# Moving five weight subtractions to GpSimd and a late table and its gathers into the first layer of expert 0

## The chip, the cores and the metric

The kernel runs on one core of a Trainium2 chip. The metric is the device time of one execution in microseconds. Five engines work side by side, each through its own instructions in order: PE (TensorE), DVE (VectorE), ACT (ScalarE), POOL (GpSimd) and SP (SyncE, which here only issues transfers). They wait for one another through semaphores.

## The reference, cut to what matters

```
state = gamma * state + k_t v_t          # retention: 4 batches, 8 heads, 768 steps, 64 wide
y_t   = scale * q_t . state
x     = y, as 3072 tokens x 512          # the input of the expert layer
e(token)    = argmax over 8 experts of the normalised logits
gate(token) = softmax weight of that expert
out[token]  = gate * ( relu(x @ w1[e]) @ w2[e] )     # w1 512x1024, w2 1024x512
```

All of it is float32; each expert works on the tokens that chose it.

## The kernel before, in words

**Retention.** Twelve blocks of 256 tokens (`m` = 0 to 11) run one after the other. In a block PE transposes the next block's q and k into PSUM, forms scores, and adds products into the two PSUM banks `py`; ACT copies the transposes to SBUF (`copy_k`, `transpose_q`) and `take(m)` copies the two banks to `yT` with three copies on ACT (L470, L473 twice). `rows(m)` turns `yT` on DVE (L478, tile `x`) and SP stores it to `xd` in HBM with four transfers (L485). `logits_products` and `logits_rows` make the expert logits of the block.

**Routing.** Blocks come in four groups of three. For a group, `sums`, `choose`, `count`, `ranks` find expert and rank of each token on DVE and PE; `split_ranks`, `marks_of`, `mark` build one-hot marks on DVE; `table` (L617) multiplies the marks on PE and DVE adds the result to `tab`, the list of tokens by expert. `counting` sorts the seven other experts by their number of tokens (`perm`, `cnti`); `sorted_tables` turns `tab` into the indices `gi` and `ri` (L716 to L729) with which GpSimd gathers rows of `xd` by indirect DMA (`gather`, L661).

**Experts.** Expert 0 is fixed as the first. Its first 288 tokens (`EARLY`) come from the first three groups and are gathered during block 10 (`early_gather`, `xge`); the other 128 (`late`) are gathered after the last table into `xr0`, together with all rows of the first sorted expert (`gather_rows(1)`), which go by `write_rows` to HBM and come back turned by `read_quarters` (`xg`), then through DVE and ACT (`x_turn`, `x_low`) to PE. Before the gathers `xr0` is cleared on POOL (L1189); it lies in memory that the retention's tiles give back.

**Weights.** Each expert's weights come in 8 pieces of 128x1024 (four of `w1`, four of `w2`) into 4 buffers `raw`. `split_cast` casts a piece to `whi` on ACT (L229) and returns a function that writes the low part `wlo = raw - whi` (L234); `split` does both. PE takes three products per matrix step, whi.xh, whi.xl, wlo.xh. `first_layer` of expert 0 is 8 times 12 products; a generator, `run(n)`, lets n of them into PE's order, so that the last group's routing stands between them. `hidden` gives `hh` (ACT, L253) and `hl` (DVE, L256); the first two `hl` are kept back in `held`. `layer2` is 24 products for each of four output parts (L1124); its step kt takes `hh`, `hl` number kt and piece 4 + kt/2.

**What sets the order.** Each engine's order is the order in which the program issues (a manual schedule). The places of the change: the branch of block 10 (`m == NM - 2`, L921 to L943) and of block 11 (L959 to L963), the end of a block (L964 to L979), the code after the blocks from L1003 on, and the start of the expert part from L1179 on.

Of the kernel before, what the change touches and what calls it, by code (L numbers as in the profile page):

```python
# [24 lines left out]
P = 128  # L25
# [7 lines left out]
NE = 8  # L33
# [78 lines left out]
def retention_moe(ctx: ExitStack, tc: tile.TileContext, q, k, v, emb, tau, w1, w2, const, const16, out):  # L112
# [351 lines left out]

    def take(m):
        yTs[m] = ap_.tile([P, KT, T2], F32, name="yT", bufs=3)
        y = yTs[m].rearrange("p (i j) (u c) -> p i (j u) c", i=2, u=2)
        at = (slice(0, 4, 2), slice(1, 4, 2)) if m % NCB else (slice(0, 4, 3), slice(1, 3))
        py = [t.rearrange("p (i j) c -> p i j c", i=2) for t in pys[m]]
        nc.scalar.copy(out=y[:, :, at[0]], in_=py[0])  # L470
        for o in range(2):

            nc.scalar.copy(out=y[o * D:(o + 1) * D, :, at[1]], in_=py[1][(1 - o) * D:(2 - o) * D])  # L473

# [236 lines left out]
    M = NE - 1  # L711
    perm = cp.tile([P, M, M], F32, name="perm")

    def sorted_tables():

        nc.vector.tensor_copy(out=ri[:, 0, 3:], in_=tab[:, 0, 2:3])  # L716
        nc.vector.tensor_copy(out=ri[:Q, 0, 3:], in_=tab[:Q, 0, 3:])
        yield
        w = ap_.tile([P, KT * P], F32, name="pm01", bufs=1)
        w = w[:, :M * NG * M].rearrange("p (m j e) -> p m j e", m=M, j=NG)  # L720
        nc.vector.tensor_tensor(out=w, in0=perm.unsqueeze(2).broadcast_to([P, M, NG, M]),
                                in1=tab[:, 1:].rearrange("p e j -> p j e").unsqueeze(1).broadcast_to([P, M, NG, M]),
                                op=ALU.mult)
        yield
        nc.vector.tensor_reduce(out=tsort, in_=w, axis=AX.X, op=ALU.add)
        yield
        nc.vector.tensor_scalar(out=gi[:, 1:], in0=tsort, scalar1=float(NT - 1), scalar2=None, op0=ALU.min)
        yield
        nc.vector.tensor_copy(out=ri[:, 1:], in_=tsort)  # L729
        yield  # L730

    def counting():
# [11 lines left out]
        yield  # L744
        pos = cp.tile([P, M], F32, name="pos")
        nc.vector.tensor_reduce(out=pos, in_=gt3, axis=AX.X, op=ALU.add)
        yield
# [107 lines left out]
    for m in range(NM):  # L855
# [3 lines left out]
        py_of(m)  # L859
        if m == NM - 2:  # L860
            first = [split_cast()]

        if m == 0:
# [36 lines left out]
        else:  # L900
# [8 lines left out]
            if urgent:  # L909
                rows(m - 1)  # L910
            if m == NM - 2:
                mark(tail - 1, range(6))
            logits_rows(m - 1, logits_products(m - 1))
            if nxt:
# [3 lines left out]
                if m == NM - 2:  # L918
# [3 lines left out]
                    state_sums(m + 1)  # L922
                    first[0]()
                transpose_q(m + 1, 0)
# [10 lines left out]
                if m == NM - 2:  # L935
                    split_cast()()
                    spread_v(m + 1, 0)
# [21 lines left out]
            else:  # L959
                lows[0]()  # L960
                intra(m, 0)
                lows[1]()
                intra(m, 1)  # L963
                ps = [turn_rows(xge, EROWS, kt, bank(f"pst{kt}")) for kt in range(2)]  # L964
        waiting = done
        take(m)
        if m < NM - 2:
            spread_v(m + 1, 0)
            spread_v(m + 1, 1)
        if m == NM - 2:  # L970
            spread_v(m + 1, 1)
            lows = [split_cast(), split_cast()]
        if m == 0:
            next(emb_steps)
        if m == NM - 1:
            xh0, xl0 = (hp.tile([P, KT, CAP], F32R, name=n) for n in ("xh", "xl"))
            for kt in range(KT):
                rows_T(xge, EROWS, kt, slice(0, EARLY), ps[kt] if kt < 2 else None)
            nc.gpsimd.tensor_copy(out=zs[0][:, :3], in_=xge[:, :, DM:DM + NE])  # L979

# [18 lines left out]
    def run(n):  # L999
        for _ in range(n):  # L1000
            next(todo, None)
# [3 lines left out]
    logits_rows(m, pl)  # L1005
    rows(m - 2)
    load_piece()
    load_piece()
    run(11)
    for j, n in EROWS[:2]:  # L1010
        square(xge, n, j, j)
    first_low = split_cast()
    z = sums(g)
    run_all(choose(g, z))
    run_all(add_counts(g, z))
    rows(m - 1)
    put_scores(g)
    run(21)
    pr = count(g)
    sort_steps = counting()  # L1020
    run_all(ranks(g, pr))
    next(sort_steps)
    for o in held:
        o()
    first_low()
    rows(m)
    square(xge, EROWS[2][1], 2, 2)
    for _ in range(9):
        next(sort_steps)
        run(1)  # L1030
    split_ranks(g)
    marks_of(g)
    for i in range(6):
        run(1)
        mark(g, (i,))
    load_expert(1)
    load_piece()
    run(4)
    split()
    load_piece()  # L1040
    load_expert(2)
    run(12)
    split()
    run(12)
    split()
    load_piece()
    load_piece()
    run(DF)
    turn_of[:] = ["b2", "b3"]

# [127 lines left out]

    def last_table():  # L1179
        table(tail)  # L1180
        run_all(sorted_tables())

    acc = layer2(0, 0, hh0, hl0, EARLY, between=last_table)
    ctxa.close()
# [7 lines left out]
    nc.gpsimd.tensor_copy(out=zs[0][:, 3], in_=xr0[:, 0, DM:DM + NE])  # L1192
    late = slice(EARLY, CAPS[0])

    def turn_late():
# [9 lines left out]
    for dt in range(3):  # L1205
        if dt:
            acc = layer2(0, dt, hh0, hl0, EARLY, between=turn_late if dt == 2 else None)
        y_turn(dt, acc, yt0, EARLY)
# [269 lines left out]
```

## Time and profile before

| what | us |
|---|---|
| median of 3 runs (lowest, highest) | 398.46 (397.87, 399.46) |
| the profiled execution, its own time | 400.53 |
| its span, first to last instruction | 398.8 |
| PE busy in the span | 386.0 |
| DVE, ACT, POOL busy | 250.2, 226.9, 125.7 |

The profiled execution took 2.07 us more than the median of the three runs; 1.73 us of it lie outside its span. A timeline row gives the start, the length, engine, line, operation, output and inputs, and in brackets the idle time in front of it with what ended it. Lengths overlap in a pipeline: two products of 288 columns that follow without a wait start 0.133 us apart though each is listed with 0.29.

### The profile page before, as it was taken

Reading aid. Unit: us, or ns where it says so; the run is one execution under the profiler, and the core shown is the slowest. Engines: PE = TensorE matmul, PEld = TensorE weight load, DVE = VectorE, ACT = ScalarE, POOL = GpSimd, SP = SyncE. Lnnn points to the kernel's source line nnn. Section 1 sums busy time; section 2 is a strip of 40 time slices with the busy share of each in tenths; the row PEclk is TensorE's granted clock in tenths of the full one; section 3 lists DMA queues with packets and bytes.
Section 4 is the critical chain, followed back from the end, with each engine's and each line's share of the span. In section 5 each row is a group of like instructions: output and inputs, shape, how many; then the busy total and the mean of one; then the engine's idle time right before and its main releaser. Section 6 shows DMA issues by size and latency. Waiting matters only on the chain.

```text
span 398.8 us, 9514 instructions
## 1 busy us (share of the span) xinstructions
PE 386.0 (97%) x3652; PEld 353.3 (89%) x3652; DVE 250.2 (63%) x564; ACT 226.9 (57%) x402; POOL 125.7 (32%) x142
## 2 busy tenths in 40 slices
PE   7999999999999998999999999999999999999992
PEld 4988888888789886999999999999889889999971
DVE  4655776779799767745773864767366547576400
ACT  5687687887974165455545655734765545453410
POOL 2765644452400434222602712420371052001131
PEclk9999999999999999999999999999999999999998
DMA  8989989999369769596979698696989687933121
GB/s 230 280 267 280 277 255 259 250 268 237 97 188 249 223 184 320 155 259 218 286 220 260 225 292 197 215 316 187 250 281 315 155 265 234 235 120 98 30 100 53
DMA packets 86470, 88.02 MB, mean 221 GB/s; under 512 B 9184, under 2 KB 65120, under 8 KB 86416
## 3 DMA queue, kind: packets, MB, share of 16 engines
q1 hardware_dynamic: 81936, 74.32, 65.8%
q0 software_dynamic: 4304, 12.93, 9.5%
q8 instruction: 31, 0.51, 0.6%
q14 instruction: 23, 0.19, 0.2%
q10 hardware_dynamic: 176, 0.07, 0.1%
HBM read 65.00 MB, written 18.43 MB: 209 GB/s over the span
## 4 chain that ended last, share of the span: by engine, by line
PE 80%; DVE 7%; DMA 6%; issue 2%; ACT 2%; POOL 1%; SPq 1%; POOLq 0%; DVEq 0%; ACTq 0%
PE pst L247 12%; PE b L247 10%; PE py L247 9%; PE py L1124 8%; PE b L1174 7%; PE py L451 7%; PE b L1124 5%; PE b L387 5%; PE pst L1124 4%; PE py L1174 4%; PE pst L421 2%; PE b L356 2%; DMA xd<-x 2%; PE b L374 2%; DMA xg<-xs 2%
## 5 line engine op out<-in xcount | busy, mean ns | idle before, releaser
L234 DVE TENSOR_TENSOR wlo<-raw,whi 128x1024 fp32r<-128x1024 f32 x64 | 78.0, 1221 | 22.8 <-ACT whi L229 17.4
L1156 POOL DMA_INDIRECT out_dram<-og,si x28 | 30.0, 1071 | 125.7 <-ACT og L1149 87.1
L229 ACT CAST whi<-raw 128x1024 fp32r<-128x1024 f32 x64 | 66.3, 1043 | 0.1
L407 DVE TENSOR_TENSOR pm<-b,mask 128x512 f32<-128x512 f32 x48 | 29.8, 684 | 13.1 <-PE b L387 13.0
L1105 DVE STREAM_TRANSPOSE xt<-xg 128x384 f32<-128x384 f32 (+1 forms) x28 | 15.7, 579 | 31.2 <-DMA xg<-xs 31.2
L661 POOL DMA_INDIRECT xr<-xd,gi x24 | 29.8, 1242 | 14.9 <-ACT sq L288 7.7
L350 POOL TENSOR_TENSOR hl<-wlo,cst 128x512 f32<-128x512 f32 x22 | 22.5, 1043 | 36.2 <-DVE pm L407 17.3
L247 PE MATMUL pst<-xl,whi 128*128 128x380 f32 (+7 forms) x96 | 32.4, 337 | 0.7 <-DVE xl L1112 0.7
L247 PE MATMUL pst<-xh,whi 128*128 128x380 f32 (+7 forms) x96 | 32.1, 335 | 0.4 <-ACT xh L1106 0.4
L247 PE MATMUL pst<-xh,wlo 128*128 128x380 f32 (+7 forms) x96 | 32.0, 333 | 0.0
L1106 ACT CAST xh<-xt 128x408 fp32r<-128x408 f32 (+6 forms) x28 | 14.2, 510 | 27.0 <-DVE xt L1105 26.7
L253 ACT ACTIVATE hh<-pst 128x380 fp32r<-128x380 f32 (+7 forms) x24 | 11.6, 484 | 28.1 <-PE pst L247 28.1
L247 PE MATMUL b<-xh,whi 128*128 128x408 f32 (+7 forms) x80 | 26.8, 335 | 0.0
L247 PE MATMUL b<-xl,whi 128*128 128x408 f32 (+7 forms) x80 | 26.7, 333 | 0.0
L247 PE MATMUL b<-xh,wlo 128*128 128x408 f32 (+7 forms) x80 | 26.6, 332 | 0.0
L247 PE MATMUL py<-xh,whi 128*128 128x288 f32 (+7 forms) x80 | 26.3, 329 | 0.0
L247 PE MATMUL py<-xh,wlo 128*128 128x288 f32 (+7 forms) x80 | 26.2, 328 | 0.0
L247 PE MATMUL py<-xl,whi 128*128 128x288 f32 (+7 forms) x80 | 26.2, 327 | 0.0
L273 POOL TENSOR_TENSOR r<-r,half 128x4 f32<-128x4 f32 (+1 forms) x9 | 8.9, 993 | 51.7 <-DVE r L272 51.6
L387 PE MATMUL b<-qT,kT 64*128 64x128 f32 x384 | 24.9, 279 | 0.0
L387 PEld LDWEIGHTS b<-qT,kT 64*128 64x128 f32 x384 | 22.6, 188 | 1.7 <-issue 0.9
L451 PE MATMUL py<-pm,vs 128*64 128x128 f32 x384 | 23.9, 276 | 0.0
(246 smaller groups left out, 1025.7 us busy)
## 6 DMA issues: line engine op xcount, KB each, us to landing
raw<-in_moe_w_dram SPq DMA_DIRECT2D x60, 512.0 KB, 4.9
whi<-in_q_dram SPq DMA_DIRECT2D x24, 256.0 KB, 4.5
xd<-x SPq DMA_DIRECT2D x48, 128.0 KB, 4.6
wlo<-in_k_dram SPq DMA_DIRECT2D x11, 512.0 KB, 5.5
xs<-xr SPq DMA_DIRECT2D x6, 768.0 KB, 4.9
whi<-in_v_dram SPq DMA_DIRECT2D x6, 512.0 KB, 5.7
wlo<-in_v_dram SPq DMA_DIRECT2D x6, 512.0 KB, 6.1
xg<-xs SPq DMA_DIRECT2D x16, 192.0 KB, 4.7
```

What stands on the lines that cost most here:

```text
L229: nc.scalar.copy(out=hv, in_=rv)
L234: eng.tensor_tensor(out=lv, in0=rv, in1=hv.bitcast(F32), op=ALU.subtract)
L247: nc.tensor.matmul(acc[:, :w], a[:, f], x[:, kt, cols], start=(n == 0), stop=(n == 3 * KT - 1))
L350: return eng.tensor_tensor(out=ks_r[:, m % 3, s, h], in0=kin[m % 3][:, h, s], in1=w[:, h], op=ALU.mult)
L387: nc.tensor.matmul(psc[a][:, j], kTs[m][a * D:(a + 1) * D, j, u].rearrange("p s c -> p (s c)"), q_cols(m, a, j, u), start=True, stop=True, ...
L407: o.append(nc.vector.tensor_tensor(out=pm, in0=psc[a], in1=w, op=ALU.mult))
L451: nc.tensor.matmul(pys[m][b][o * D:(o + 1) * D, j], lhsT, rhs, start=first, stop=True, skip_group_check=True)
L661: return nc.gpsimd.indirect_dma_start(out=xr[:n, j, :], out_offset=None, in_=xd[:rows_, :], in_offset=bass.IndirectOffsetOnAxis(ap=gi[:n, ...
L1105: nc.vector.transpose(out=xt[:, :n], in_=xgs[e][:, :n, kt * Q:(kt + 1) * Q])
L1124: nc.tensor.matmul(acc[:, :c], a[:, f], x[:, kt, :c], start=(n == 0), stop=(n == 3 * FT - 1))
L1156: i = nc.gpsimd.indirect_dma_start(out=out[:, :], out_offset=bass.IndirectOffsetOnAxis(ap=si[:n, e, j:j + 1], axis=0), in_=og[:n, j, :], i ...
L1174: nc.tensor.matmul(acc[:s, :], x[:, kt, at], a, start=(n == 0), stop=(n == 3 * FT - 1))
```

## The change

It leaves the arithmetic as it is and changes who does it, and when.

- In blocks 10 and 11 the first expert's piece 0 is cast after block 11's transposes instead of before them; piece 1 is cast after `take(10)`; pieces 1 and 3 get their low parts on POOL. `take(11)` does its two half copies on DVE.
- The low parts of pieces 4, 5 and 6 go to POOL too; piece 2 and piece 7 stay on DVE.
- `rows(9)` moves into block 11, `rows(10)` ahead of the last choice; the marks of the last group come ahead of the held `hl` and of `rows(11)`.
- The last `table` and `sorted_tables` move from the first part of layer 2 (behind its 18th product) to behind the 72nd product of the first layer; the clearing of `xr0` and the five gathers come directly after it. `perm` lies in PSUM now.
- The sort that gives `cnti`, and with it the loads of expert 1's first four pieces, come after the gathers.

```diff
-    def take(m):
+    def take(m, copy=nc.scalar.copy):
...
-            nc.scalar.copy(out=y[o * D:(o + 1) * D, :, at[1]], in_=py[1][(1 - o) * D:(2 - o) * D])
+            copy(out=y[o * D:(o + 1) * D, :, at[1]], in_=py[1][(1 - o) * D:(2 - o) * D])
...
-    perm = cp.tile([P, M, M], F32, name="perm")
+    perms = []
...
+        perm = pc[:, P:P + M * M].rearrange("p (m e) -> p m e", m=M)
+        perms.append(perm)
...
-        if m == NM - 2:
-            first = [split_cast()]
...
+            if not nxt:
+                rows(m - 2)
...
-                    first[0]()
...
-                    split_cast()()
+                    split()
...
-                lows[0]()
+                second_low()
                 intra(m, 0)
-                lows[1]()
                 intra(m, 1)
...
-        take(m)
+        take(m, nc.scalar.copy if nxt else nc.vector.tensor_copy)
...
         if m == NM - 2:
+            split(nc.gpsimd)
             spread_v(m + 1, 1)
-            lows = [split_cast(), split_cast()]
+            second_low = split_cast()
...
         if m == NM - 1:
+            nc.gpsimd.tensor_copy(out=zs[0][:, :3], in_=xge[:, :, DM:DM + NE])
+            split(nc.gpsimd)
...
-    rows(m - 2)
     load_piece()
     load_piece()
+    rows(m - 1)
     run(11)
...
-    first_low = split_cast()
+    turn_of[:] = ["b2", "b3"]
+    split(nc.gpsimd)
     z = sums(g)
...
-    rows(m - 1)
     put_scores(g)
-    run(21)
+    run(16)
     pr = count(g)
     sort_steps = counting()
     run_all(ranks(g, pr))
-    next(sort_steps)
+    for _ in range(5):
+        next(sort_steps)
+    square(xge, EROWS[2][1], 2, 2)
+    split_ranks(g)
+    marks_of(g)
+    mark(g, range(6))
     for o in held:
         o()
-    first_low()
     rows(m)
...
+    run(21)
+    split(nc.gpsimd)
     run(12)
-    split()
+    split(nc.gpsimd)
     run(12)
...
+    last_low = split_cast()
...
-    acc = layer2(0, 0, hh0, hl0, EARLY, between=last_table)
+    table(tail)
+    run_all(sorted_tables())
...
     gather_rows(1)
...
+    run(12)
+    last_low()
+    for _ in range(4):
+        next(sort_steps)
+    load_expert(1)
+    load_piece()
+    load_piece()
+    load_expert(2)
+    load_piece()
+    load_piece()
+    run(DF)
```

ACT, blocks 10 and 11, from the copies of `take(9)` and `spread_v` on (`whi` is a cast piece, `kT` and `qT` the turned k and q, `vs` the spread v). Before:

```order
L400 COPY vs<-whi 64x512 x4
L229 CAST whi<-raw 128x1024
L361 COPY kT<-b_1985 128x8x64
L375 COPY qT<-b_2021 128x512
L375 COPY qT<-b_2027 128x512
L361 COPY kT<-b_2033 128x8x64
L229 CAST whi<-raw 128x1024
L400 COPY vs<-wlo 64x512 x2
L470 COPY yT<-py_1907 128x4x128
L473 COPY yT<-py_1908 64x4x128 x2
```

And with the change:

```order
L400 COPY vs<-whi 64x512 x4
L361 COPY kT<-b_1981 128x8x64
L375 COPY qT<-b_2016 128x512
L375 COPY qT<-b_2022 128x512
L361 COPY kT<-b_2028 128x8x64
L229 CAST whi<-raw 128x1024
L400 COPY vs<-wlo 64x512 x2
L470 COPY yT<-py_1906 128x4x128
L473 COPY yT<-py_1907 64x4x128 x2
L229 CAST whi<-raw 128x1024
```

One of the two casts ahead of `take(10)` has moved behind it.

POOL, from the early gathers of block 10 to the late ones (`zs` are scores of the gathered rows, `xr` the late rows), as a difference:

```order
 L661 DMA xge<-xd,ri 128x520 x2
 L661 DMA xge<-xd,ri 32x520
-L979 COPY zs_82<-xge 128x24
-L1189 MEMSET xr_2490 128x520
-L661 DMA xr_2490<-xd,ri 128x520
+L234 TENSOR_TENSOR wlo<-raw,whi 128x1024
+L976 COPY zs_82<-xge 128x24
+L234 TENSOR_TENSOR wlo<-raw,whi 128x1024
+L234 TENSOR_TENSOR wlo<-raw,whi 128x8x4x32 x3
+L1174 MEMSET xr_2396 128x520
+L661 DMA xr_2396<-xd,ri 128x520
```

Five subtractions of a whole piece stand ahead of the clearing and the late gathers.

DVE, from the last group's marks on (`hl` low parts of the hidden layer, `tab` the table, `ri` indices). Before:

```order
L609 TENSOR_SCALAR pm_2322<-cst_62,low 128x128 x6
L256 SCALAR_TENSOR_TENSOR hl<-pst_2305,hh 128x288
L234 TENSOR_TENSOR wlo<-raw,whi 128x8x4x32
L256 SCALAR_TENSOR_TENSOR hl<-b_2355,hh 128x288
L234 TENSOR_TENSOR wlo<-raw,whi 128x8x4x32
L256 SCALAR_TENSOR_TENSOR hl<-b_2386,hh 128x288
L234 TENSOR_TENSOR wlo<-raw,whi 128x8x4x32
L256 SCALAR_TENSOR_TENSOR hl<-py_2405,hh 128x288
L256 SCALAR_TENSOR_TENSOR hl<-py_2428,hh 128x288
L622 TENSOR_TENSOR tab<-tab,b_2462 128x32
L623 TENSOR_TENSOR tab<-tab,b_2462 128x32
L716 CAST ri<-tab 128x1
```

And with the change:

```order
L609 TENSOR_SCALAR pm_2288<-cst_62,low 128x128 x6
L256 SCALAR_TENSOR_TENSOR hl<-py_2204,hh 128x288
L256 SCALAR_TENSOR_TENSOR hl<-py_2241,hh 128x288
L478 STREAM_TRANSPOSE x<-yT 128x4x4x32 x2
L256 SCALAR_TENSOR_TENSOR hl<-pst_2255,hh 128x288
L256 SCALAR_TENSOR_TENSOR hl<-pst_2320,hh 128x288
L256 SCALAR_TENSOR_TENSOR hl<-b_2339,hh 128x288
L622 TENSOR_TENSOR tab<-tab,b_2374 128x32
L623 TENSOR_TENSOR tab<-tab,b_2374 128x32
L716 CAST ri<-tab 128x1
```

Three subtractions of weights are gone from between marks and table, and the turn of `rows(11)` has come in. The five `hl` there are now the first to the fifth; the other three and one subtraction stand behind the indices.

## Rows read from the trace of the kernel before

**Rows 1.** Timeline of ACT, block 10.

```profile
99.39 1.05 ACT L229 CAST whi<-raw 128x1024 fp32r<-128x1024 f32 x1
```

**Rows 2.** Timeline of PE, block 11 to the first product of expert 0.

```profile
106.71 1.09 PE L451 MATMUL py<-qT,s 64*64 64x128 f32 x28 [0.39 <-ACT yT L473]
...
112.37 0.64 PE L498 MATMUL b<-yT,enT 128*32 128x256 f32 x8
112.94 0.40 PE L247 MATMUL py<-xh,whi 128*128 128x288 f32 x1
```

**Rows 3.** Timeline of PE, layer 2 of expert 0, parts 0 to 2, and what follows.

```profile
126.54 0.30 PE L1124 MATMUL pst<-hh,whi 128*128 128x288 f32 x1
...
129.20 0.40 PE L1124 MATMUL pst<-hh,wlo 128*128 128x288 f32 x1 [0.44 <-DVE wlo L234]
...
131.07 0.40 PE L1124 MATMUL pst<-hl,whi 128*128 128x288 f32 x1 [0.57 <-DVE hl L256]
...
138.74 0.40 PE L1225 MATMUL b<-whi,xh 128*128 128x512 f32 x1
```

**Rows 4.** Timeline of DVE, the last group's ranks, marks and table.

```profile
118.08 0.21 DVE L567 TENSOR_TENSOR rs<-b,oh 128x48 f32<-128x48 f32 x1
...
118.52 0.81 DVE L256 SCALAR_TENSOR_TENSOR hl<-py,hh 128x288 fp32r<-128x288 f32 x2
...
120.38 1.30 DVE L478 STREAM_TRANSPOSE x<-yT 128x512 f32<-128x512 f32 x2
121.60 0.12 DVE L739 SCALAR_TENSOR_TENSOR key<-cnt,cst 128x8 f32<-128x8 f32 x1
...
122.49 0.21 DVE L753 TENSOR_TENSOR gt<-perm,cst 128x49 f32<-128x49 f32 x1
...
123.48 0.16 DVE L579 TENSOR_TENSOR ge<-rank,cst 128x18 f32<-128x18 f32 x1
...
125.09 1.06 DVE L609 TENSOR_SCALAR pm<-cst,low 128x128 f16<-128x128 f16 x6
...
131.30 0.18 DVE L622 TENSOR_TENSOR tab<-tab,b 128x32 f32<-128x32 f32 x1
```

**Rows 5.** Timeline of POOL, clearing and last late gather.

```profile
133.17 0.53 POOL L1189 MEMSET xr<- 128x520 f32 x1 [24.56 <-DMA raw<-in_moe_w_dram]
...
139.26 0.92 POOL L661 DMA_INDIRECT xr<-xd,gi  x1 [0.30 <-issue]
```

**Rows 6.** Chain that ended last, expert 1's rows: start, length, what.

```profile
147.03 6.17 DMA xg<-xs
```

**Rows 7.** Timeline of PE, the start of expert 1.

```profile
153.70 0.40 PE L1174 MATMUL pst<-wlo,hh 128*128 128x512 f32 x1
154.51 0.45 PE L247 MATMUL pst<-xh,whi 128*128 128x408 f32 x1 [0.41 <-ACT xh L1106]
...
158.54 0.35 PE L247 MATMUL b<-xh,whi 128*128 128x408 f32 x1
```

**Rows 8.** The page, part 5: a GpSimd subtraction's nearest relative, busy and mean ns.

```profile
L350 POOL TENSOR_TENSOR hl<-wlo,cst 128x512 f32<-128x512 f32 x22 | 22.5, 1043 | 36.2 <-DVE pm L407 17.3
```

**Rows 9.** Timelines of POOL and of DVE, the same stretch.

```profile
143.22 0.20 POOL L1084 COPY zs<-xr 128x24 f32<-128x24 f32 x1 [1.14 <-DMA xr<-xd,gi]
143.91 0.65 POOL L1086 COPY zs<-xr 32x8 f32<-32x8 f32 x1 [0.49 <-DMA xr<-xd,gi]
...
143.29 1.22 DVE L234 TENSOR_TENSOR wlo<-raw,whi 128x1024 fp32r<-128x1024 f32 x1 [2.35 <-ACT whi L229]
```

**Rows 10.** Timeline of SP: stores of block 11, loads of expert 1.

```profile
121.70 2.62 SPq L485 DMA_DIRECT2D xd<-x  x4
125.46 5.55 SPq L204 DMA_DIRECT2D raw<-in_moe_w_dram  x4
```

**Rows 11.** Tile `xd`: stores issued 115.2 to 116.6, their landing.

```profile
DMA to landing us min/median/max: 2.0/2.1/2.2
```

**Rows 12.** Tile `xd`: stores issued 123.3 to 123.8, their landing.

```profile
DMA to landing us min/median/max: 3.9/3.9/3.9
```

More of the change, by code (lines that the diff above doesn't have):

```diff
@@ L720, in sorted_tables @@
         w = w[:, :M * NG * M].rearrange("p (m j e) -> p m j e", m=M, j=NG)
-        nc.vector.tensor_tensor(out=w, in0=perm.unsqueeze(2).broadcast_to([P, M, NG, M]),
+        nc.vector.tensor_tensor(out=w, in0=perms[0].unsqueeze(2).broadcast_to([P, M, NG, M]),
                                 in1=tab[:, 1:].rearrange("p e j -> p j e").unsqueeze(1).broadcast_to([P, M, NG, M]),
@@ L978, in retention_moe @@
                 rows_T(xge, EROWS, kt, slice(0, EARLY), ps[kt] if kt < 2 else None)
-            nc.gpsimd.tensor_copy(out=zs[0][:, :3], in_=xge[:, :, DM:DM + NE])
         for _ in range(LOADS.count(m)):
@@ L1021, in retention_moe @@
     run_all(ranks(g, pr))
-    next(sort_steps)
+    for _ in range(5):
[4 more added lines that the diff above has]
+    mark(g, range(6))
     for o in held:
         o()
-    first_low()
     rows(m)
[L1027 to L1038, printed above, removed]
-    split()
-    load_piece()
-    load_expert(2)
+    run(21)
+    split(nc.gpsimd)
     run(12)
-    split()
+    split(nc.gpsimd)
     run(12)
[L1045 to L1049, printed above, removed]
+    last_low = split_cast()
     xgs, xTs, xrs = {}, {}, {}
@@ L1176, in layer2_rows @@
         return acc
-    def last_table():
-        table(tail)
-        run_all(sorted_tables())
-    acc = layer2(0, 0, hh0, hl0, EARLY, between=last_table)
+    table(tail)
+    run_all(sorted_tables())
     ctxa.close()
@@ L1205, in retention_moe @@
     for dt in range(3):
-        if dt:
-            acc = layer2(0, dt, hh0, hl0, EARLY, between=turn_late if dt == 2 else None)
+        acc = layer2(0, dt, hh0, hl0, EARLY, between=turn_late if dt == 2 else None)
         y_turn(dt, acc, yt0, EARLY)
```

## The prediction

> **What bounds the kernel now.** I read the page first. PE is busy 386.0 of 398.8 us (the table above), so only time in which PE waits, or work taken off it, can bring anything; this change takes no product off PE. So I went through PE's timeline from block 10 to expert 1 and looked for rows with a bracket, or for starts further apart than 0.133 us. There are three places.
>
> First, ahead of block 11's products PE waits for ACT's copies of `take(10)`: the bracket [rows 2]. ACT is late because two casts of weights stand ahead of those copies; the reader sees the first, 1.05 us, before the copy of `kT` [rows 1].
>
> Second, layer 2 of expert 0. Its first three parts run from 126.54 to 138.74 [rows 3], 12.20 us. They hold 72 products at 0.133 us, 9.60, the four transposes of the late rows, 0.44 with their gap, and the last table, 0.19. That leaves 1.97 us of waiting, shown by the brackets on `wlo` and `hl`, both of DVE. DVE is the late one: between 126.4 and 131.3 it does three weight subtractions with `hl` between them, and then the table.
>
> Third, expert 1. Its first product could follow the row at 153.70 by 0.23 us, at 153.93, and twelve products of 0.184 us would bring the next group to 156.14. It starts at 158.54 [rows 7]: 2.40 us lost, with `xh` and `xl` of expert 1's rows as the releasers. The chain of waits says why: their last transfer lands at 147.03 + 6.17 = 153.20 [rows 6]. Back along it stand the last gather, issued at 139.26, and the clearing of `xr` at 133.17 [rows 5], which starts when DVE has made the indices. So the table's place sets when expert 1 can start.
>
> **The change, part by part.**
>
> *Casts.* One cast of 1.05 us leaves the front of block 11's transposes. PE's transposes were done some 0.2 us before ACT was free to copy them, and that is all that is gained: `take(10)` comes 0.2 us sooner, since its other cast still stands ahead. The first product of expert 0 goes from 112.94 [rows 2] to 112.75.
>
> *`take(11)` on DVE.* The trace has no such copy. The half copies cost 0.58 us each on ACT, and a DVE operation of 512 columns from PSUM is the nearest relative of that size; I take 0.6 each, with 0.58 and 0.7 as ends. ACT's third cast ends near 109.7, DVE's subtraction behind it (1.22 listed [rows 9], 1.15 in a train) at 110.9, the copies at 112.1. The logits start at 112.37 before [rows 2], 112.17 now. So this is hidden with less than 0.1 us to spare, and costs 0 to 0.2.
>
> *Five subtractions on POOL.* The nearest row is a GpSimd subtraction's relative of half the width, 1043 ns [rows 8]; twice that is 2.05 us (lower end 2.0; upper end 2.7, where POOL also waits 0.65 for DVE [rows 9]). The fourth piece is cast by 111.3, so its low part ends at 113.4 and is wanted by the twelfth product at 114.3. Those of pieces 4, 5, 6 run at about 115.0 to 117.0, 119.9 to 121.9, 121.9 to 124.0; layer 2 wants the last at 128.4. All are covered, and POOL had nothing to do there: it waited 24.56 us [rows 5]. At 2.7 us still only the fourth piece comes near its product.
>
> *DVE without them.* From ranks to marks the path is 0.44 (118.08 to 118.52), 0.89 (121.60 to 122.49) and 2.67 (123.48 to 126.15) [rows 4], 4.0 us. Starting at 117.05 the marks end at 121.1. Two `hl` (0.72), the turn of `rows(11)` (1.22) and three `hl` (1.1) follow, to 124.15. PE makes the table after 72 products, at 123.15, so DVE is the later one and starts `tab` at 124.15. Table to indices takes 133.17 - 131.30 = 1.87 [rows 4, 5]: indices at 126.05. Then one `hl`, the one subtraction left (1.15, to 127.6), the sort for `cnti` (to 128.3), the last two `hl` (to 129.1). PE starts layer 2 at 126.54 - 0.2 + 0.19 = 126.53 and wants the sixth `hl` at 128.7 (there at 126.4), the last subtraction at 129.2 and the seventh `hl` at 129.1 (there at 128.65), the eighth at 129.5. So the 1.97 us of waiting go. What is late next is that seventh `hl`, with 0.4 us to spare. Together with the 0.2, PE is 2.15 us ahead at 136.6.
>
> *Gathers.* The clearing also waits for the stores of `rows(11)`, whose tile it overwrites: turned by 123.1, issued within 2.1, landed 2.0 to 3.9 us later [rows 10 to 12]. That gives 127.2 to 129.1. The stores at 115.2 had few others beside them and so do these, whose loads now come later; I take 127.4. The last gather follows 6.09 behind (133.17 to 139.26), at 133.5, and the landing of expert 1's rows 13.94 behind that (139.26 to 153.20), at 147.4, or at 149.1 with the late stores.
>
> *Expert 1.* DVE can turn those rows only after the fourth subtraction for expert 1, which ends at 151.37 before and 149.2 now. From the landing at 153.20 to the second group at 158.54 it was 5.34 us [rows 6, 7]; from 149.2 this gives 154.5 against 156.14 - 2.15 = 154.0 for PE alone. So 0.5 of the 2.40 stays, and 1.9 go.
>
> *Not on the path.* The loads of expert 1's pieces are issued from 125.46 before [rows 10]; now they follow `cnti` and two register loads, from about 130 to 132. Their first cast is wanted at 136, and DVE and ACT have 6 us between them and PE there. SP has nothing behind them that is ready sooner than the gathers' rows.
>
> **Sum.** 0.2 + 1.95 + 1.9 = 4.05, less up to 0.1 for the copies: 4.0 us. The profiled execution took 400.53, so 396.5 for it; it stood 2.07 above the median of the runs, and the sum taken from 398.46 is **394.5 us**.
>
> **Rivals.**
>
> *DVE and POOL hold each other up.* POOL's copy of 32x8 took 0.65 us though the larger one just before took 0.20, and it ended at 144.56, right behind the DVE subtraction from 143.29 to 144.51 [rows 9]. So the two do wait for one another. The trace has no DVE operation with two SBUF inputs that meets a long POOL one; the change brings one such meeting, POOL's low part of piece 5, from 119.9, and the marks, to 121.1. If POOL gets in between, the marks end at 123.1 and all of DVE behind them is 2.0 later; the seventh `hl` comes at 130.6 for 129.1, and 1.5 us of waiting return, while expert 1 still starts well. Then 4.0 - 1.5 = 2.5, 395.9 us. If the same happens with the next piece too, PE waits for the table itself, 2.1, and then 1.6 for `hl`: with the other gains about 398.3. Against both: the marks may already be running, and POOL then waits, which costs nothing. The Trainium skill speaks against the change here: "SBUF — State Buffer", section "Who interferes with whom", calls the port pair of the two engines an exclusive lock, held for a whole instruction, for DVE operations with two SBUF inputs against GpSimd ones that read SBUF. By that rule the short copy [rows 9] lost the port to DVE, and what matters is who issues first; by it the sum would be between 394.5 and 398.3.
>
> *Expert 1 does not start sooner.* If some other link (the cast and subtraction of the fourth piece, a late row) holds it, the 1.9 stays lost: 396.4 us. For it: DVE's place for the turn has only 0.5 to give. Against: the landing moves by nearly 6 us and needs 4.
>
> *Loads against gathers: slower.* Expert 1's four loads, 2 MB, ran ahead of the gathers; now they are issued beside them, at 130 to 132 against 127 to 134. The last quarter of expert 1's rows took 6.17 to land [rows 6] with other loads beside it. If the gathers and what follows lose more than 1.8 us by this, expert 1 waits for them one for one; from 5.8 on it starts later than before. Were they held for all the loads, about 8 us, the rows would land at 155.4 and the second group start at 160.7: 2.2 slower, 400.7 us. Against: the same loads were in flight ahead of the first gathers before, and the gathers move only half as many bytes.
>
> *It does not do what it says.* Were the clearing held by the stores until 133, nothing of the third place would come; their landing speaks against it [rows 11, 12].
>
> **How the numbers follow.** The forecast gets 0.52, the lock once 0.22, expert 1 not sooner 0.12, the lock twice 0.08, the loads 0.06. Half a per cent, 2.0 us, is about what a measurement here can tell from no change, so 396.5 is the border. Forecast and lock once lie below it, expert 1 not sooner lies on it: faster 0.77, same 0.16, slower 0.07. The range runs from 393.8 (the 0.5 at expert 1 gone too, with 0.2 more in block 11) to 396.9 (expert 1 not sooner, with 0.5 for the copies and the spread of runs).
>
> **What would show it.** Right: no bracket on `wlo` or `hl` in layer 2 of expert 0, late rows reached near 136.6; clearing near 127.4; expert 1's rows landed by 149; its second group near 154.5. Lock: a mark or `eq` on DVE that takes 2 us, or a subtraction on POOL well above 2.1. Wrong: a bracket in the first layer on the fourth piece's `wlo`, a table that PE waits for, or rows of expert 1 landing after 151.

## The result, and the profile after

The changed kernel took a median of **402.59 us** (402.28 to 405.56, 5 runs) against 398.46 (397.80 to 399.46, 5 runs): a ratio of 1.0119 with a 95% interval of 1.0079 to 1.0160 (worked out from all runs; the two medians alone give 1.0104). It is slower by about 1%, clear of noise, where 394.5 us was forecast. The profiled execution took 403.63 us, its span 401.8.

Six starts on PE cut each execution into stages: the first logits product of block 10, the first product of expert 0, the first of its layer 2, the first of its late rows, the first of expert 1's second group, and the end of the span. The stages can be compared between executions; where block 10 begins cannot, since it varied by some us between executions that had done the same work until then.

| us | blocks 10, 11 | layer 1 | layer 2, parts 0 to 2 | to expert 1's second group | rest |
|---|---|---|---|---|---|
| before (the execution of the prediction) | 14.07 | 13.60 | 12.20 | 19.80 | 240.26 |
| before, another execution | 14.08 | 13.60 | 12.30 | 18.06 | 240.34 |
| changed | 14.58 | 18.09 | 10.02 | 18.59 | 240.59 |

Layer 1 grew by 4.49 us; that is the result. Layer 2 lost 2.18 to 2.28, as was forecast. The rows of the changed kernel follow, first DVE's timeline of the last marks and the first `hl` behind them (start, length, engine, line, operation, tiles, count):

```profile
121.99 5.37 DVE L609 TENSOR_SCALAR pm<-cst,low 128x128 f16<-128x128 f16 x6
127.28 0.81 DVE L256 SCALAR_TENSOR_TENSOR hl<-py,hh 128x288 fp32r<-128x288 f32 x2
```

Beside them POOL, the low parts of pieces 5 and 6, and later the clearing and the last gather:

```profile
121.80 4.86 POOL L234 TENSOR_TENSOR wlo<-raw,whi 128x1024 fp32r<-128x1024 f32 x2 [3.08 <-issue]
...
133.54 0.54 POOL L1174 MEMSET xr<- 128x520 f32 x1 [6.89 <-DMA xd<-x]
...
139.63 0.91 POOL L661 DMA_INDIRECT xr<-xd,gi  x1 [0.30 <-issue]
```

The marks took 1.06 us before [rows 4] and take 5.37 now. The first two have 2.41 and 2.39 us each, as long as a subtraction on POOL (2.43 here, 2.37 to 2.40 where one stands alone); POOL's first began 0.19 us ahead of them. The other four take 0.25 us each. So each of two marks waited for a whole subtraction.

PE of the changed kernel, the table and what follows it, the start of layer 2, of the late rows and of expert 1's second group:

```profile
124.92 0.20 PE L617 MATMUL b<-pm,pm 128*128 128x64 f16 x1
126.77 0.85 PE L617 MATMUL b<-pm,pm 128*128 128x64 f16 x5 [1.64 <-DVE pm L609]
127.78 0.40 PE L247 MATMUL py<-xh,whi 128*128 128x288 f32 x1 [0.16 <-DVE hl L256]
...
132.60 0.29 PE L1112 MATMUL pst<-hh,whi 128*128 128x288 f32 x1
...
142.62 0.40 PE L1220 MATMUL b<-whi,xh 128*128 128x512 f32 x1
...
161.21 0.34 PE L247 MATMUL b<-xh,whi 128*128 128x408 f32 x1
```

The table's second product waits for the second mark, and the first layer goes on at 127.78 instead of 125.1 (the table's six products take 0.19 us where nothing is late): 2.7 us. In layer 2 the brackets on `wlo` and `hl` [rows 3] are gone. Then the clock, by stretches of the changed kernel (stretch, its length, busy time and count for PE, PEld, DVE, ACT and POOL, the granted clock, DMA share and GB/s):

```profile
124.00:126.00 2.00, 1.12 (x10) 0.94 (x8) 2.00 (x2) 1.27 (x2) 2.00 (x2) 1.00 0.00 0
126.00:127.50 1.50, 0.73 (x5) 0.47 (x5) 1.50 (x6) 0.00 (x0) 0.66 (x1) 1.00 0.00 0
127.50:128.40 0.90, 0.74 (x5) 0.63 (x6) 0.90 (x3) 0.00 (x0) 0.00 (x0) 0.90 0.00 0
128.40:131.40 3.00, 3.00 (x14) 3.00 (x14) 2.90 (x10) 0.41 (x1) 0.00 (x0) 0.50 0.31 72
```

From 128.4 to 131.4, after that wait, PE has half its clock (0.50, the 1.2 GHz level), though it is busy throughout; its products of 288 columns start 0.24 us apart there for 0.133. Thirteen of them cost 13 x 0.107 = 1.4 us. So 2.7 + 1.4 = 4.1 of layer 1's 4.49 are named; 0.19 more are the table, which stood in layer 2 before.

The clock's share is that of this execution: of the five, two had a mean clock of 0.996 and 0.997 and took 402.59 and 402.44 us all the same. The last two `hl` on DVE say why that can be:

```profile
134.20 0.80 DVE L256 SCALAR_TENSOR_TENSOR hl<-py,hh 128x288 fp32r<-128x288 f32 x2
```

An estimate from this row and those of PE: DVE works without a gap from its marks to the last `hl` at 135.00, and has the seventh `hl` at about 134.6; PE asks for it 19 products, 2.5 us, into layer 2. With its full clock PE would have begun layer 2 about 1.4 us sooner, at 131.2, and would have waited there some 0.9 us for that `hl`. So, by the estimate, the clock adds only about 0.5 us to what DVE's delay costs anyway.

Blocks 10 and 11, on PE and then on DVE:

```profile
107.76 1.09 PE L451 MATMUL py<-qT,s 64*64 64x128 f32 x28 [0.53 <-ACT yT L473]
...
113.94 0.64 PE L498 MATMUL b<-yT,enT 128*32 128x256 f32 x8 [0.46 <-ACT xh L682]
114.51 0.40 PE L247 MATMUL py<-xh,whi 128*128 128x288 f32 x1
```

```profile
112.41 1.39 DVE L473 COPY yT<-py 64x512 f32<-64x512 f32 x2
```

The bracket on `yT` is 0.53 where it was 0.39 [rows 2], and block 11's logits start right after DVE's second half copy (112.41 + 1.39 = 113.80), though their bracket names ACT's `xh`.

Last, the chain of waits of the changed kernel, from the stores of `rows(11)` to expert 1's rows (start, length, what):

```profile
130.68 2.55 DMA xd<-x
...
139.63 7.38 DMA xr<-xd,gi
147.03 2.08 DMA xs<-xr
...
150.66 5.18 DMA xg<-xs
```

The clearing waited for those stores (133.54 and 6.09 behind it the last gather, as forecast), and all of it stood as late as before [rows 5], since the marks were late. The last gather took 7.38 us to land; before, its rows were landed and stored again within 4.6 (from 139.26 [rows 5] to the last store at 143.87).

### The profile page after: what moved, and what is told of

It is laid out like the page before. It is cut to its first block, busy times and chain, and to the rows that moved or that the text cites. A ratio compares the mean times of both kernels' runs of the same rounds, so it can differ in the third digit from the quotient of the medians.

```text
span 401.8 us, 9516 instructions
## 1 busy us (share of the span) xinstructions
PE 388.2 (97%) x3652; PEld 355.5 (88%) x3652; DVE 250.6 (62%) x561; ACT 226.2 (56%) x400; POOL 137.7 (34%) x147
## 4 chain that ended last, share of the span: by engine, by line
PE 77%; DMA 8%; DVE 7%; issue 2%; SPq 2%; ACT 1%; POOL 1%; POOLq 0%; DVEq 0%; ACTq 0%
PE pst L247 11%; PE b L247 9%; PE py L247 8%; PE py L1112 7%; PE b L1162 7%; PE py L451 6%; PE b L1112 5%; PE pst L1112 4%; PE py L1162 4%; PE b L387 4%; DMA xd<-x 4%; PE pst L421 2%; PE b L356 2%; DMA xr<-xd,gi 2%; PE b L374 2%
## 5 line engine op out<-in xcount | busy, mean ns | idle before, releaser
L234 DVE TENSOR_TENSOR wlo<-raw,whi 128x1024 fp32r<-128x1024 f32 x59 | 72.0, 1220 | 26.8 <-ACT whi L229 21.5
L247 PE MATMUL py<-xh,whi 128*128 128x288 f32 (+7 forms) x80 | 27.2, 340 | 0.2 <-DVE hl L256 0.2
L253 ACT ACTIVATE hh<-py 128x288 fp32r<-128x288 f32 (+7 forms) x20 | 9.5, 473 | 27.9 <-PE py L247 27.9
```

What stands on the lines that cost most here:

```text
L234: eng.tensor_tensor(out=lv, in0=rv, in1=hv.bitcast(F32), op=ALU.subtract)
L247: nc.tensor.matmul(acc[:, :w], a[:, f], x[:, kt, cols], start=(n == 0), stop=(n == 3 * KT - 1))
L253: nc.scalar.activation(out=hh[:, ft, cols], in_=acc[:, :w], func=AF.Relu)
```

## The experiments

The theory after the result: GpSimd holds DVE up at the marks, twice, and PE pays with its wait for the table and with its clock. Rivals: DVE's copies in block 11; the subtraction on GpSimd in itself; loads beside the gathers. Ratios are to the kernel before on the same chip, with their 95% intervals.

| run | median us (runs) | ratio | blocks | layer 1 | layer 2 | to expert 1 | rest |
|---|---|---|---|---|---|---|---|
| e1_gate | 399.39 (10) | 1.0021 [0.9990, 1.0052] | 14.58 | 13.84 | 10.03 | 18.98 | 240.62 |
| e2_gate6 | 400.48 (10) | 1.0045 [1.0026, 1.0063] | 14.58 | 14.42 | 11.19 | 18.77 | 240.63 |
| e3_actcopies | 403.24 (4) | 1.0110 [1.0088, 1.0132] | 14.28 | 18.28 | 10.03 | 18.83 | 241.98 |
| e4_before_low5 | 400.31 (10) | 1.0062 [1.0024, 1.0100] | 14.05 | 13.61 | 12.94 | 18.08 | 240.27 |
| e5_gate_act | 398.88 (12) | 1.0007 [0.9985, 1.0029] | 14.29 | 14.37 | 10.02 | 18.82 | 240.66 |
| e6_early_loads | 399.60 (12) | 1.0025 [1.0003, 1.0046] | 14.29 | 14.37 | 11.39 | 17.82 | 240.61 |
| e7_before_low4 | 398.56 (12) | 0.9992 [0.9969, 1.0014] | 14.06 | 13.60 | 11.46 | 18.34 | 240.29 |
| e8_before_low45 | 399.38 (12) | 1.0004 [0.9984, 1.0024] | 14.06 | 13.60 | 12.12 | 18.02 | 240.26 |
| e9_act_sort | 398.77 (12) | 0.9988 [0.9966, 1.0009] | 14.28 | 14.38 | 10.15 | 17.80 | 240.63 |
| e10_old_blocks | 397.72 (12) | 0.9948 [0.9924, 0.9972] | 14.07 | 13.85 | 10.29 | 17.77 | 241.19 |

### The meeting at the marks: e1_gate, e2_gate6, e3_actcopies

e1_gate is the changed kernel with the low parts of pieces 5 and 6 held back on GpSimd until the last mark; e2_gate6 holds back piece 6 alone. `after(a, b)` makes a wait for b; that `mark` and `split` return their last instruction for it is left out below.

```diff
-    mark(g, range(6))
+    marked = mark(g, range(6))
...
-    split(nc.gpsimd)
+    after(split(nc.gpsimd), marked)
     run(12)
-    split(nc.gpsimd)
+    after(split(nc.gpsimd), marked)
```

> The changed kernel, with one thing added: GpSimd's low parts of pieces 5 and 6 wait for the last of the six marks. Theory (the two engines hold each other up: each of the first two marks stood 2.4 us behind a GpSimd subtraction, PE then waited for the table and its clock fell to 0.50 behind that wait): the six marks take 1.06 us again instead of 5.37, PE does not wait for them, no granted clock of 0.5 behind the table, and the time is 395.5 us, 394.5 to 397, some 7 us under the changed kernel. Rival (the marks are late for another reason, or the loss comes from the copies in block 11 or from the loads beside the gathers): the time stays at 401 to 403.

> The changed kernel, with only the low part of piece 6 waiting for the last mark, so that one meeting is left. Theory: one mark takes 2.4 us, the other five 0.25 each, the marks end about 2.1 us sooner than in the changed kernel; PE waits for the table 0.3 to 0.6 instead of 1.64 us, and if the clock falls only behind the long wait it stays at 1.0: 396.5 to 399 us. Rival (what is lost is not lost meeting by meeting): 401 to 403.

e3_actcopies is the changed kernel with block 11's half copies back on ACT.

```diff
-        take(m, nc.scalar.copy if nxt else nc.vector.tensor_copy)
+        take(m)
```

> The changed kernel with the two half copies of the last block's result back on ScalarE. Theory: only block 11 moves, by the 0.5 us that the first product of expert 0 came later than worked out; the marks still meet the two subtractions, and the time is 401.5 to 403, about the changed kernel's. Rival (the copies on VectorE are what delays all that follows on VectorE): 399 or less, with the marks ended 2 us or more sooner.

DVE's marks in e1_gate and in e2_gate6, one timeline each:

```profile
120.88 1.06 DVE L610 TENSOR_SCALAR pm<-cst,low 128x128 f16<-128x128 f16 x6
```

```profile
123.47 3.21 DVE L610 TENSOR_SCALAR pm<-cst,low 128x128 f16<-128x128 f16 x6
```

Held back, the marks take 1.06 us as before the change; with one subtraction beside them 3.21, with two 5.37 (5.39 in e3_actcopies). Each meeting adds 2.15 us to DVE. What it costs is not the same each time. With one (400.48 us, where 396.5 to 399 was expected) the ratio goes from 1.0021 to 1.0045, 1 us: in the traces layer 1 grows by 0.58 us and layer 2 by 1.16, since all of DVE is later, but PE waits only 0.16 for an `hl` in layer 1 and 0.91 for one in layer 2, and the granted clock stays at 1.00. With the second the ratio is 1.0119, 3 us more: layer 1 grows by another 3.67 us, and layer 2 gives 1.17 back, since PE comes to it later. In e3_actcopies (403.24 us, just above the 401.5 to 403 expected) the wait at the table was 1.59 us and the granted clock was 0.50 from 126.4 to 129.4, behind it. So there the mechanism is the changed kernel's, and the half copies are worth 0.3 us in blocks 10 and 11 (14.28 for 14.58). That the meeting at the marks makes the change slower is shown; of the price, e1_gate against the changed kernel gives 3.8 us by the stages and 3.9 by the ratios.

But e1_gate is no faster than the kernel before, where 395.5 us was expected of it. Its layer 2 is 2.2 us shorter, and it gives 0.5 back in blocks 10 and 11, 0.24 in layer 1 (0.19 of it the table), 0.9 on the way to expert 1 (against the second execution of before) and 0.3 in the rest. The next runs went after these.

### Only the meeting, in the kernel before: e4_before_low5

```diff
     run(4)
-    split()
+    split(nc.gpsimd)
```

> The kernel before, with one thing changed: the low part of piece 5 is done by GpSimd, beside VectorE's sort and marks. Theory: a VectorE operation with two inputs in SBUF, or a mark, that meets it takes about 2.4 us instead of 0.2; VectorE saves one subtraction of 1.15 later, so the table comes about 1 us later and the time is 398.5 to 400.5. Rival (no holding up): all VectorE rows keep their lengths, VectorE's train is 1.15 us shorter, and the time falls to 396.8 to 397.8.

DVE, then POOL, in this run:

```profile
122.57 0.20 DVE L746 TENSOR_REDUCE pos<-gt 128x7 f32<-128x49 f32 x1
122.81 2.06 DVE L748 TENSOR_TENSOR perm<-pos,cst 128x49 f32<-128x49 f32 x1
```

```profile
122.39 2.41 POOL L234 TENSOR_TENSOR wlo<-raw,whi 128x1024 fp32r<-128x1024 f32 x1 [13.99 <-ACT whi L229]
```

Here no mark is met; it is the equality test `perm`, with two inputs in SBUF, that takes 2.06 us for 0.21, while the reduction in front of it, which began 0.18 us after POOL, is not held. DVE is spared 1.22 us and loses 1.85; layer 2 becomes 0.64 to 0.74 us longer, and the kernel slower.

### How much there was to gain at expert 1: before_again, e5_gate_act, e6_early_loads

before_again is the kernel before, unchanged, in one more profiled execution (399.77 us).

> The kernel before, unchanged, profiled once more. The profiled execution that the prediction read took 400.53 us, 2.07 more than the median of its runs. If its stages are what every execution has, the stretch from the logits of block 10 to the second product group of expert 1 is again 59.7 us (98.87 to 158.54) and what differs lies before it, in the retention blocks: 57 to 60 us there would still be called the same only within 0.3. Rival: the stretch itself was 1 to 2 us longer in that one execution, above all the wait at the start of expert 1, and so part of the forecast gain was never there in the others.

The way from the late rows to expert 1's second group took 18.06 us in it, where the execution behind the prediction shows 19.80. By the prediction's own count 17.40 of it is work (19.80 less 2.40), so the wait was 0.66 us here. Three runs that differ from the kernel before only ahead of that stage agree with it: 18.08 in e4_before_low5, 18.34 and 18.02 in the two runs of the next section that start from that kernel. Most of the 2.40 belonged to that one execution.

e5_gate_act is e1_gate with the half copies on ACT; e6_early_loads is e5_gate_act with the sort and three of expert 1's loads ahead of the last table, and the turn of `rows(11)` ahead of the held `hl`.

```diff
+    rows(m)
     for o in held:
         o()
-    rows(m)
...
     after(split(nc.gpsimd), marked)
     run(12)
+    for _ in range(4):
+        next(sort_steps)
+    load_expert(1)
+    load_piece()
+    load_piece()
+    load_piece()
     last_low = split_cast()
```

> The kernel of the first run (GpSimd's low parts of pieces 5 and 6 behind the marks), with the last block's two half copies back on ScalarE. Theory: those copies cost 0.3 us ahead of expert 0 (14.58 to 14.28 from the logits of block 10 to its first product): about 399.0 us, 398 to 399.6. Rival: no difference from the first run, 399.4 or more.

> As the run before it, and the sort that names expert 1 and the loads of three of its pieces moved ahead of the table, the turn of the last block's rows ahead of the two held low parts. Theory (the second half of the missing gain: the loads run beside the late gathers, whose last one landed 7.9 us after its issue instead of 4.6): the loads start near 127 instead of 130.3, the last gather lands in 4.6 to 6.5 us, expert 1 starts 1 us sooner: 398.0 us, 397 to 398.8. Rival (the gathers are slow for another reason): they still land 7.5 to 8 us after issue, and the time is that of the run before.

e5_gate_act matches the kernel before. The first product of expert 0 comes 0.3 us sooner than in e1_gate, but layer 1 is 0.53 longer: its first product waits 0.16 for `xh`, the second starts 0.49 behind it for 0.24, and the third 0.23 behind that for 0.13; the rest of the 0.53 was not followed up. So the copies on ACT give nothing that the stages show.

SP and the chain of e5_gate_act, then SP of e6_early_loads:

```profile
129.76 2.95 SPq L204 DMA_DIRECT2D raw<-in_moe_w_dram  x4
137.38 3.99 SPq L1062 DMA_DIRECT2D xs<-xr  x3
141.53 0.33 SPq L1066 DMA_DIRECT2D xs<-xr  x1
```

```profile
133.68 7.83 DMA xr<-xd,gi
141.53 2.23 DMA xs<-xr
```

```profile
128.33 2.81 SPq L204 DMA_DIRECT2D raw<-in_moe_w_dram  x4
138.97 1.31 SPq L1068 DMA_DIRECT2D xs<-xr  x3
140.32 0.45 SPq L1072 DMA_DIRECT2D xs<-xr  x1
```

In e6_early_loads the first load is issued 7.34 us ahead of the last gather (128.33, 135.67), and the last store follows that gather by 4.65 us; in e5_gate_act the loads begin 3.92 ahead of it, and the store follows by 7.85. The stores of `rows(11)`, whose turn moved too, are issued at 123.4 in both, so they are not the difference. So the rival "loads against gathers" is real, 3.2 us on the gather; the way to expert 1 shrinks from 18.82 to 17.82 without it. Yet the run gained nothing, where 397 to 398.8 us was expected, because layer 2 grew by 1.37. DVE of e6_early_loads says why:

```profile
125.49 0.14 DVE L761 COPY esort<-cst 128x1 f32<-128x1 f32 x1
125.67 1.56 DVE L766 CAST cnti<-esort 1x8 int32<-1x8 f32 x1
127.15 0.17 DVE L624 TENSOR_TENSOR tab<-tab,b 128x32 f32<-128x32 f32 x1
```

A cast of eight numbers takes 1.56 us (0.16 in the kernel before), until POOL's second subtraction ends (122.43 + 4.77 = 127.20): a third place where the two engines meet, and the table is queued behind it.

### The meeting moved again, and avoided: e7_before_low4, e8_before_low45, e9_act_sort

e7_before_low4 and e8_before_low45 start from the kernel before.

```diff
-    first_low = split_cast()
+    split(nc.gpsimd)
...
-    first_low()
```

> The kernel before with one low part alone on GpSimd, piece 4's, cast just ahead of the last group's choice. Theory (only a GpSimd subtraction beside a DVE operation of the blocking kind costs): it runs from about 115.5 to 117.9 beside DVE operations that were not held at that place in the runs so far; DVE's train behind it is 1.14 us shorter, so the brackets in layer 2 shrink and layer 2 up to the late rows takes about 11.1 us for 12.2; the median comes out some 1 us below the kernel before. Rival (what layer 2 gains is given back at expert 1, whose rows and weights come when they come): layer 2 shortens alike, the stretch from the late rows to the second group of expert 1 grows from 18.1 to about 19, and the median is that of the kernel before. Second rival (one more meeting): a DVE row of 0.2 us in 115.5 to 118 takes 1 to 2 us, and the median is 0.5 to 1.5 above.

e8_before_low45 adds, as in e1_gate, the hold behind the last mark:

```diff
-        mark(g, (i,))
+        marked = mark(g, (i,))
...
     run(4)
-    split()
+    after(split(nc.gpsimd), marked)
```

> As the run before, and piece 5's low part on GpSimd too, behind the last mark. Theory: DVE's train is 2.3 us shorter, no operation is held, layer 2 up to the late rows takes about 10.2 us, no bracket there; the last gather is issued some 2 us sooner, with the loads still ahead of the gathers, so its rows take about 4.6 us to land and expert 1 starts no later against the late rows than by 0.7: median 1.3 to 2 us below the kernel before. Rival (given back at expert 1): layer 2 10.2, the stretch behind it 19.5 or more, median within 0.5 of the kernel before. If tab or perm beside the subtraction are held, a row of DVE above 2 us shows it.

Piece 4 alone on GpSimd takes 0.74 to 0.84 us out of layer 2 and the median moves by 0.65 (0.9992, and the interval holds 1): the direction of the theory, in a size this measurement doesn't tell from nothing. Piece 5 beside it gives even that back. DVE of e8_before_low45:

```profile
125.68 3.07 DVE L234 TENSOR_TENSOR wlo<-raw,whi 128x1024 fp32r<-128x1024 f32 x1
```

Its own subtraction of piece 6 (1.22 alone) now meets POOL's of piece 5 (125.27 to 127.68): DVE is spared 1.22 and loses 1.85, and layer 2 is at 12.12. The expectation of 10.2 missed this; it had looked at marks, `perm` and `tab`, and not at the subtraction next door.

e9_act_sort is e6_early_loads with the cast of eight numbers on ACT.

```diff
-        nc.vector.tensor_copy(out=cnti[:, :NE], in_=es[:1])
+        nc.scalar.copy(out=cnti[:, :NE], in_=es[:1])
```

> The last kernel with early loads, with one change: the cast of the sorted order to integers (1x8) is done by ACT instead of DVE, where it took 1.56 us beside GpSimd's low part of piece 6 and 0.16 elsewhere. Theory: the table comes 1.4 us sooner, the bracket of 0.65 on hl in layer 2 of expert 0 goes, layer 2 takes 10.0 us for 11.4, and the stretch from the late rows to the second group of expert 1 stays at 17.8 to 18.3: median 0.9 to 1.4 us below that kernel's 399.6. Rival (the 1.56 was a wait for another thing, such as SP's reading of the order): the table stays where it was, layer 2 at 11.4, same median. Second rival: the 1.4 us are lost again at expert 1, where the stretch becomes 19.2.

Layer 2 went from 11.39 to 10.15 and the way to expert 1 stayed at 17.80: the 1.56 us were the meeting, and what it cost came back. Its ratio is 0.9988 for 1.0025, so 1.5 us less by the ratios (each to the kernel before on its own chip).

### Blocks 10 and 11 as before: e10_old_blocks

e9_act_sort with the casts of pieces 0 to 3 where the kernel before has them, and their low parts on DVE again.

```diff
+        if m == NM - 2:
+            first = [split_cast()]
...
+                    first[0]()
...
-                    split()
+                    split_cast()()
...
-                second_low()
+                lows[0]()
                 intra(m, 0)
+                lows[1]()
                 intra(m, 1)
...
-            split(nc.gpsimd)
             spread_v(m + 1, 1)
-            second_low = split_cast()
+            lows = [split_cast(), split_cast()]
...
-            nc.gpsimd.tensor_copy(out=zs[0][:, :3], in_=xge[:, :, DM:DM + NE])
-            split(nc.gpsimd)
...
+            nc.gpsimd.tensor_copy(out=zs[0][:, :3], in_=xge[:, :, DM:DM + NE])
```

> The kernel with early loads and the sort's cast on ACT, with the changes in blocks 10 and 11 undone: the first four pieces are cast and subtracted where the kernel before does it (all on DVE). What the change does there was forecast to gain 0.2 us; in the kernels with it the first product of expert 0 comes 0.2 us (copies on ACT) to 0.5 us later against block 10's logits, and its products then start in two steps of 0.49 and 0.23. Theory (these moves cost, they don't gain): first product at +14.07 as before, layer 1 13.8 (0.19 more than before, for the table that now stands in it), 10.1 and 17.8 behind it: 0.8 us less than the kernel it is made from, median some 1 to 1.3 us below the kernel before. Rival (DVE is late in layer 1 once the four subtractions stand ahead of it again): first product at +14.07, but a bracket in layer 1 or on the table, and no gain over 398.8.

**397.72 us, 0.9948 [0.9924, 0.9972]: this kernel is half a per cent faster than the kernel before**, and so faster than the changed one. The ratio gives 2.1 us; the stages of its one trace add up to 1.2 us less than those of before's second execution, and where the rest lies is not shown. Blocks and layer 1 together take 27.92 us for 28.66 in e9_act_sort; the table accounts for 0.19 of what is left over the 27.67 of before. Its POOL and DVE around the table, then PE at layer 2 and the late rows:

```profile
115.69 2.39 POOL L234 TENSOR_TENSOR wlo<-raw,whi 128x1024 fp32r<-128x1024 f32 x1 [6.81 <-ACT whi L229]
122.06 4.79 POOL L234 TENSOR_TENSOR wlo<-raw,whi 128x1024 fp32r<-128x1024 f32 x2 [3.98 <-ACT whi L229]
127.27 0.53 POOL L1184 MEMSET xr<- 128x520 f32 x1 [0.41 <-DVE ri L731]
```

```profile
120.77 1.06 DVE L610 TENSOR_SCALAR pm<-cst,low 128x128 f16<-128x128 f16 x6
```

```profile
127.15 0.30 PE L1122 MATMUL pst<-hh,whi 128*128 128x288 f32 x1
...
137.44 0.40 PE L1224 MATMUL b<-whi,xh 128*128 128x512 f32 x1
```

Three subtractions on POOL, none beside an operation that it holds, clearing as soon as the indices are there. In its profile 0.85 us are lost again behind expert 1's start (241.19 for 240.34), 0.6 of them one wait for a `wlo`; whether that belongs to this kernel or to this execution was not tried.

## Why the prediction was wrong

**Two engines meet twice at the marks.** The step that failed is "The trace has no DVE operation with two SBUF inputs that meets a long POOL one; the change brings one such meeting" and, from it, the chance of 0.08 for the lock twice. The rival was right in mechanism, place and count ("PE waits for the table itself, 2.1, and then 1.6 for `hl`"), and nearly in its price: 3.7 us, where the stages of e1_gate and the changed kernel differ by 3.8. In the profiled execution this came as 2.7 us of waiting in layer 1 and 1.4 of a slower clock, which no term had, in place of the wait for `hl` in layer 2. Its 398.3 (398.2 by its own terms) was 4 us too low because it counted "the other gains", which did not come either, as told below. It was meant to be rare for a wrong reason: "the marks may already be running, and POOL then waits, which costs nothing". POOL began 0.19 us ahead of the marks in the changed kernel, and its next subtraction started between the first mark and the second.

The first half of that sentence was also wrong about the trace that the prediction read. There POOL and DVE meet early in the retention; the third row is the same addition in e1_gate:

```profile
13.01 2.05 POOL L345 TENSOR_TENSOR hh<-whi,cst 128x512 f32<-128x512 f32 x2
14.10 0.97 DVE L279 TENSOR_TENSOR r<-r,r 8x1 f32<-8x1 f32 x1
14.82 0.15 DVE L280 TENSOR_TENSOR r<-r,r 8x1 f32<-8x1 f32 x1
```

DVE adds two operands of 8x1 in SBUF and takes 0.97 us, until POOL's second multiplication ends at 15.06; in e1_gate, where it starts behind that multiplication, it takes 0.15. The price of a meeting could be read before the change was made.

The prediction looked at two SBUF inputs, and the marks have one (a constant row; `low` is a scalar for each partition). The runs show which DVE operations of this kernel a subtraction on POOL held: `TENSOR_SCALAR` of 128x128 (2.41 for 0.25), `TENSOR_TENSOR` with two inputs in SBUF (`perm` 2.06 for 0.21, `wlo` 3.07 for 1.22), and the cast of 1x8 (1.56 for 0.16). Not held were reductions, transposes, `hl` and `tab` (one input in PSUM), and copies and casts of one element a row. The Trainium skill has this in the very section that the prediction named ("SBUF — State Buffer", "Who interferes with whom"): besides two SBUF inputs it names copy, cast and tensor_scalar, which can enter a mode that uses two ports and can then contend, and says of reductions that on trn2 they never contend. The traces agree on tensor_scalar, on the cast and on the reductions (0.20 us beside POOL as alone, in e4_before_low5); of copies they show only one of 128x1 beside a subtraction, and that was not held (0.14 us in e6_early_loads). The sentence on tensor_scalar was the one to apply to the marks.

**Subtractions on POOL.** 2.37 to 2.43 us for the forecast 2.05, inside its bounds of 2.0 to 2.7. None was late for PE; the size of the error did no harm.

**Layer 2.** Right: no brackets, 10.02 us where 12.20 - 1.97 - 0.19 = 10.04 follows from its count. In the changed kernel PE comes to it late, which hides DVE's delay; that it holds without this is shown by e1_gate, 10.03.

**The casts.** Wrong in sign. "`take(10)` comes 0.2 us sooner" failed: with its cast gone, ACT sat idle ahead of the first copy of `kT` until PE had its transposes, the copy came 0.15 us sooner, and that was gone again by the other cast, which starts 3.78 us after block 10's first logits in both. Block 11 then lost 0.5: ACT's third cast ended 0.4 later than assumed, and DVE's half copies, behind the subtraction that waits for that cast, took 0.69 each for 0.6. e10_old_blocks shows the moved casts and low parts to be a loss: undone, with the half copies on ACT in both kernels, blocks and layer 1 take 0.74 us less.

**Expert 1.** "So 0.5 of the 2.40 stays, and 1.9 go" failed twice over. The 2.40 were read from one execution; another has 0.66 to give. And the loads did lengthen the last gather. In e1_gate, where the table is early, it is issued at 134.22 (forecast 133.5) but lands in 7.90 us; expert 1's rows arrive at 150.94, 3.5 behind the forecast 147.4, and the wait is 1.6 us. The prediction's own rule for loads against gathers, one for one beyond 1.8, gives 1.7. The mechanism was there, at a chance of 0.06; what it took away was a gain that the kernel before mostly did not have to give.

**The sum.** Of the forecast 4.0, the 2.2 in layer 2 came. Against before's second execution, e1_gate gives back 0.5 + 0.24 + 0.92 + 0.28 = 1.94 and keeps 2.27 - 1.94 = 0.33, which a measurement here cannot tell from nothing, and the interval of its ratio indeed holds 1. The meeting added 3.8 to 3.9 us on top. So of the 8.1 us between forecast and result about half is the meeting, and 4.0 - 0.33 = 3.7 are gains that did not come or were given back; 0.6 is not traced.

## What to carry to other kernels

Before work is given to GpSimd, list what DVE runs beside it, operation by operation: here operations with two SBUF inputs, a scalar operation and a cast from SBUF to SBUF were each held until GpSimd's instruction ended, and reductions, transposes and operations that read PSUM were not. Place long GpSimd instructions, by a dependency, where DVE runs the second kind; left to the order alone, they found a new neighbour each time (marks, `perm`, `cnti`, `wlo`). And read a wait of one or two us from two executions before it is entered in a sum.

## What the runs showed of the hardware

- What a meeting costs depends on how much slack PE has, and not on DVE's delay alone: 2.15 us on DVE cost 1 us with one meeting and 3 us more with the second, when PE's wait in layer 1 grew from 0.16 us to 1.64 and the granted clock behind it was 0.50 for 3 us.
- The DVE operation that is held need not be long: an addition of 8x1 took 0.97 us beside a GpSimd multiplication of 1.05, and 0.15 alone.
- Five gathers that were issued with 2 MB of loads in the same 5 us had the last one stored again 7.4 to 7.9 us after its issue (changed kernel, e1_gate, e5_gate_act), against 4.6 where the loads were issued ahead of the gathers (kernel before, e6_early_loads).
